# A Fourier mix in front of an MLP: the sum along the sequence of the third and fourth batch as a DFT of length six over the chunks

## The chip, the cores and the metric

The kernel runs on one core of one Trainium2 chip. The metric is the device time of one execution in microseconds. TensorE is called PE, VectorE DVE, ScalarE ACT, GpSimd POOL, and SyncE, which issues most transfers, SP.

## The reference

There are four batches. In each, a recurrent attention with decay (8 heads, 768 positions, 64 values a head) gives `x` of 768 x 512. Then comes a Fourier mix and an MLP:

```
X = np.fft.fft(x, axis=1)
X = np.fft.fft(X, axis=2)
u = x + np.real(X)
un = (u - mean(u)) / sqrt(var(u) + 1e-6)
out = u + relu(un @ w_ch1) @ w_ch2
```

The first transform runs along the 768 positions, the second along the 512 columns. The real part needs the cosine and the sine sums along the sequence, for frequencies 0 to 384; the others mirror them.

## The kernel before, in words

Position = 128 * chunk + row, with six chunks and the 128 rows on the partitions. `x16` holds x in f16, each chunk in two halves: columns 0 to 255 and columns 256 to 511 in reversed order, so that a column and its mirror stand at the same place.

**Attention of one batch** goes in steps over four pairs of heads. `cast_unit` (POOL), `t_unit` (transposes), `kv_unit` (products of keys and values, L683, and VectorE's running sums `s`, L693), `a_unit` (scores, PE L664; the mask is put on by VectorE, L667, giving `atm`, in three parts of two chunks) and `y_unit`: PE takes `s` (L714) and then `atm` (L718) into two PSUM banks, and ScalarE evicts them into `x16` (L726).

**The fold.** `fold_s` (L743) makes sums and differences of chunk c and chunk c + 3: `ab[:, parity, c, half, column]`. Even frequencies need the sums, odd ones the differences. It runs twice for a batch: on columns 0 to 129 of either half when the third pair of heads is done, on the rest after the fourth pair. `fold_d` (L770) folds the two halves into `eo` (sum for the cosine, difference for the sine), `fold_e` (L784, L786) folds once more into `ee`. What is left for each of the four column groups (`e` for cosine or sine, `cb`) is a sum over three chunks of 128 rows for each parity: `s1_unit` (L847) does it with three matmuls of 193 columns a parity, the tables `csp` and `ssp` on the moving side, into a PSUM bank of two blocks; ScalarE evicts the bank into `g`, putting even and odd frequencies in turn, and VectorE writes the mirror `gr` (L858). `g0_unit` (L874 to L900) makes the sum of column 0 by itself: two small VectorE operations, nine matmuls of 4 columns (L891), two small VectorE operations.

**The second transform and the norm.** `s2_unit` (L1009 to L1039) contracts `g` with tables along the columns for blocks `kb` of 128 frequencies, and `norm_unit` and `unT_unit` make the normalised, transposed input of the MLP.

**The MLP** is done in two halves `rt` of 384 positions: sixteen `h_unit` (four matmuls of 384 columns each, L1087, into one of three PSUM banks; the eviction with the Relu is on ScalarE, L1091, for the numbers in `ACT_ROWS`, else on VectorE, L1093), then three output blocks of sixteen matmuls (L1130), each evicted by VectorE (L1134) and sent out by SP.

**The order of the work.** The first batch up to its norm has an order written out by hand (`FIRST`). Behind that, `emit` merges streams of units: each stream has a start and an end on an axis on which batch b's MLP takes b to b + 1, its units are spread evenly between them, and all units are emitted by that place. The constants `DM1`, `TS1`, `DA1`, `LD1` give the starts and ends. While batch b's MLP runs, batch b + 1's attention, fold and first half of the mix run beside it. Each engine then takes its instructions strictly in the emitted order and waits for what each one needs.

Of the kernel before, what the change touches and what calls it, by code (L numbers as in the profile page):

```python
# [11 lines left out]
AF = mybir.ActivationFunctionType  # L12
# [7 lines left out]
P = 128  # L20
B, H, S, D = 4, 8, 768, 64
DM = 512
# [24 lines left out]
"""  # L47
ON_ACT = {'q': (0, 1, 0), 'kv': (1, 1, 1), 'g': (0, 1, 1), 'gr': (0, 0, 0)}
FB = 1
DM0, DM1 = (0.183, 0.205, 0.286, 0.408), (0.004, 0.137, 0.232, 0.341)  # L50
TS0 = (0.228, 0.358, 0.398, 0.465, 0.512, 0.573, 0.684, 0.694)
TS1 = (-0.040, -0.020, 0.048, 0.585)
DA0, DA1 = (0.043, 0.161, 0.176, 0.190, 0.284, 0.321), (0.063, 0.067, 0.063, 0.158, 0.168, 0.189)
LD0, LD1 = (0.223, 0.312), (-0.370, 0.140)
HT0 = (0.666, 0.693, 0.632, 0.590)
NPE = 2
KD = (2, 3)
NT = 0.6
ACT_ROWS = ((2, 5, 6, 7, 8, 9, 10, 14), (0, 3, 6, 7, 9, 10, 11, 12, 14, 15), (2, 4, 5, 6, 7, 8, 10, 11, 13, 14))


@with_exitstack
def kernel(
# [668 lines left out]
    def fold_s(b, lo, hi, s0, s1):  # L732
        def run():
            x = xts[b % 2]
            if b not in fd:
                fd[b] = dict(
                    ab=fp.tile([P, 2, 3, 2, XW], f16, tag="xab", name="xab"),
                    eo=fp.tile([P, 2, 2, 3, 256], f16, tag="eo", name="eo"),
                    g=gp.tile([P, 4, KN], f16, tag="g16", name="g16"),
                    gr=gp.tile([P, 4, 384], f16, tag="g16r", name="g16r"))  # L740
            ab = fd[b]["ab"]
            for a, op in ((0, ALU.add), (1, ALU.subtract)):
                nc.vector.tensor_tensor(out=ab[:, a, :, s0:s1, lo:hi],  # L743
                                        in0=x[:, 0:3, s0:s1, lo:hi],
                                        in1=x[:, 3:6, s0:s1, lo:hi], op=op)
        return run
# [18 lines left out]
    def fold_d(b, cb, es=(0, 1)):  # L765
# [7 lines left out]
                                        op=(ALU.add, ALU.subtract)[e])  # L773
        return run

    def fold_e(b, e):
        def run():
            eo = fd[b]["eo"]
            if e == 0:
                fd[b]["ee"] = fp.tile([P, 4, 2, 3, 128], f16, tag="xab", name="ee",  # L780
                                      padded_shape=[P, 4, 2, 3, 130])
            ee = fd[b]["ee"]
            lo, hi = eo[:, e, :, :, 0:128], eo[:, e, :, :, 254:126:-1]
            nc.vector.tensor_tensor(out=ee[:, 2 * e], in0=lo, in1=hi,  # L784
                                    op=ALU.add if e == 0 else ALU.subtract)
            nc.vector.tensor_tensor(out=ee[:, 2 * e + 1], in0=lo, in1=hi,  # L786
                                    op=ALU.subtract if e == 0 else ALU.add)
            if e == 0:
                nc.vector.tensor_copy(ee[:, 1, :, :, 127:128], eo[:, 0, :, :, 255:256])
        return run  # L790
# [49 lines left out]
    def s1_unit(b, e, cb):  # L840
        def run():
            eo, g, gr = fd[b]["eo"], fd[b]["g"], fd[b]["gr"]
            tab = csp if e == 0 else ssp
            ps = ps_g.tile([P, 2, NK], f32, tag="g", name="ps1", padded_shape=[P, 2, 256])
            for par in range(2):
                for sb in range(3):
                    nc.tensor.matmul(ps[:, par, :],  # L847
                                     fd[b]["ee"][:, 2 * e + cb, par, sb, :] if b >= FB else
                                     eo[:, e, par, sb, 128 * cb:128 * cb + 128],
                                     tab[:, par, sb, :], start=(sb == 0), stop=(sb == 2))  # L850
            gi = 2 * e + cb
            dst = g[:, gi].rearrange("p (i t) -> p t i", t=2)
            if e == 0 or ON_ACT["g"][min(b, 2)]:
                nc.scalar.copy(dst, ps)
            else:
                nc.vector.tensor_copy(dst, ps)
            if b:
                (nc.scalar.copy if ON_ACT["gr"][min(b, 2)] else nc.vector.tensor_copy)(  # L858
                    gr[:, gi], g[:, gi, 384:0:-1])
        return run  # L860
# [4 lines left out]
    def g0_unit(b, parts=(0, 1, 2)):  # L865
        def run():
            for part in parts:
                (g0_a, g0_b, g0_c)[part](b)
        return run
# [212 lines left out]
    def h_unit(b, rt, fb):  # L1082
        def run():
            unT = lb[b]["unT"]
            psh = ps_pm.tile([P, 384], f32, tag="pm", name="psh", padded_shape=[P, DM])
            for cb in range(4):
                nc.tensor.matmul(psh, w116[:, cb, fb * P:(fb + 1) * P],  # L1087
                                 unT[:, cb, rt * 384:(rt + 1) * 384],
                                 start=(cb == 0), stop=(cb == 3))
            if fb in ACT_ROWS[2 if (b, rt) == (B - 1, 0) else rt]:  # L1090
                nc.scalar.activation(ht16[:, fb, :], psh, AF.Relu, bias=0.0, scale=-1.0)  # L1091
            else:
                nc.vector.tensor_scalar(out=ht16[:, fb, :], in0=psh, scalar1=-1.0, scalar2=0.0,  # L1093
                                        op0=ALU.mult, op1=ALU.max)
        return run
# [61 lines left out]
    def attn_steps(b):  # L1157
        steps = []
        for step in range(6):
            un = []  # L1160
            if step < 4:
                un.append(held(cast_unit(b, step)))
            i = step - 1
            if 0 <= i < 4:
                un.append(kv_unit(b, i))
            i = step - 2
            if 0 <= i < 4:
                un.append(y_unit(b, i))
                if i == 2:
                    un += [fold_s(b, 0, 130, 0, 2), fold_d(b, 0)]  # L1170
                    if b < FB:
                        un += [g0_unit(b), s1_unit(b, 0, 0), s1_unit(b, 1, 0)]
            if step < 4:
                un.append(t_unit(b, step))
            i = step - 1
            if 0 <= i < 4:
                if b == 0:
                    un += [a0_unit(b, i, 0), a0_unit(b, i, 1)]
                else:
                    un += [a_unit(b, i, part) for part in range(3)]  # L1180
            if step == 5:
                un += [fold_s(b, 130, 258, 0, 2), fold_d(b, 1)]
                if b >= FB:
                    un += [g0_unit(b), fold_e(b, 0), fold_e(b, 1)]
            steps.append(un)
        return steps

# [88 lines left out]
    for b in range(B):  # L1276
        majors = []
        if b == 0:
            for kb in range(3):
                if kb:  # L1280
                    majors.append(unT_unit(0, kb))
                majors += [h0_unit(kb, g) for g in range(4)]
        else:
            majors += [h_unit(b, 0, fb) for fb in range(NFB)]
        majors.append(rstd_unit(b, 0))
        majors += [ch_unit(b, 0, rb3, part) for rb3 in range(3) for part in range(4)]
        majors += [h_unit(b, 1, fb) for fb in range(NFB)]
        majors.append(rstd_unit(b, 1))
        majors += [ch_unit(b, 1, rb3, part) for rb3 in range(3) for part in range(4)]
        streams.append((majors, b, b + 1.0))  # L1290
        streams += mix_units(b, [3, 4, 5], *(b + t for t in (DM0 if b == 0 else DM1)))
        if b + 1 < B:
            steps = attn_steps(b + 1)
            if b == 0:
                streams.append(([load_unit(1, i, 6) for i in range(4)], LD0[0], LD0[1]))
                streams.append(([qt_zeros], 0.1, 0.15))
                streams.append(([half_tables], HT0[0], HT0[1]))
                streams.append(([pad_unit], HT0[2], HT0[3]))
                ts = TS0
            else:  # L1300
                streams.append(([load_unit(b + 1, i) for i in range(4)], b + LD1[0], b + LD1[1]))
                n = [len(u) for u in steps[1:]]
                ts = list(TS1[:2]) + [TS1[2] + TS1[3] * sum(n[:j]) / sum(n) for j in range(6)]
            streams.append((steps[0], b + ts[0], b + ts[1]))
            streams += [(u, b + ts[j + 2], b + ts[j + 3]) for j, u in enumerate(steps[1:])]
            end = b + ts[-1]
            da = DA0 if b == 0 else DA1
            streams.append(([s1_unit(b + 1, e, cb) for cb in range(2) for e in range(2)
                             if cb or b + 1 >= FB], end + da[0], end + da[1]))
            streams += mix_units(b + 1, [0, 1, 2], *(end + t for t in da[2:]))  # L1310
# [31 lines left out]
```

## Time and profile before

| what | value |
|---|---|
| median of three runs | 242.17 us (241.97 to 242.35) |
| the profiled execution | 242.19 us |
| its span, first to last instruction | 240.2 us |
| PE busy | 228.5 us, 1999 matmuls |
| VectorE busy | 172.8 us |
| ScalarE busy | 120.8 us |
| granted TensorE clock, mean | 1.000 |

The profile has one row for each group of instructions, by line of the kernel before. The chain of waits is followed back from the last instruction: each piece has its start, its length and what ran. The timeline has start, length, engine, line and operation, and in brackets the idle time ahead and what ended it. Matmuls overlap, so that the mean of one is longer than the step from one to the next.

### The profile page before, as it was taken

To read this page: it belongs to the slowest core of one execution; us is meant where nothing else is said; L and a number is where in the kernel's file an instruction comes from. 1 tells how busy PE (TensorE), PEld (TensorE's weight loads), DVE (VectorE), ACT (ScalarE), POOL (GpSimd) and SP (SyncE) were. 2 spreads that over 40 slices of the span, in tenths; PEclk is the share of its full clock that TensorE was granted. 3 is DMA by queue.
4 is the path that set the end of the run, shared out by engine and by line. 5 is a ranking of instruction groups with operands and counts; after the bars stand their busy time and mean duration, and the time that the engine had idled before them with its cause. 6 is when DMAs were issued, how large, how long until landed. Compare 5 with 4: busy or idle time off the path is not lost.

```text
span 240.2 us, 5238 instructions
## 1 busy us (share of the span) xinstructions
PE 228.5 (95%) x1999; PEld 142.6 (59%) x1999; DVE 172.8 (72%) x419; ACT 120.8 (50%) x268; POOL 81.6 (34%) x148
## 2 busy tenths in 40 slices
PE   0888999999999999999999999999999999999994
PEld 0366779756774646665557446655675455446543
DVE  8789987968898789977995749977886557315121
ACT  5989759674865544941248406722366227203400
POOL 8377802675300097850001808930003224000000
PEclk9999999999999999999999999999999999999999
DMA  7999999999999399979999587675100331221012
GB/s 179 232 271 266 209 206 207 209 246 247 233 231 216 65 202 217 192 142 136 257 275 208 106 182 207 130 117 153 44 3 0 84 115 23 44 90 44 1 44 87
DMA packets 100808, 36.77 MB, mean 153 GB/s; under 512 B 91440, under 2 KB 97840, under 8 KB 100784
## 3 DMA queue, kind: packets, MB, share of 16 engines
q1 hardware_dynamic: 96560, 32.25, 63.7%
q0 software_dynamic: 4224, 4.19, 10.5%
q8 instruction: 15, 0.25, 0.4%
q14 instruction: 9, 0.07, 0.1%
HBM read 27.26 MB, written 6.29 MB: 140 GB/s over the span
## 4 chain that ended last, share of the span: by engine, by line
PE 83%; DVE 5%; SPq 5%; DMA 3%; POOL 2%; ACT 1%; issue 1%; ACTq 0%; POOLq 0%; DVEq 0%
PE psc L1130 34%; PE psh L1087 28%; SPq L216 5%; PE psh L1104 3%; PE wkA L664 3%; DMA q<-in_q_dram 3%; PE ps L847 3%; PE wkY L718 2%; PE pq L1009 2%; PE wkY L714 1%; PE wkK L683 1%; PE ps L827 1%; PE tq L620 1%; PE pst L1074 1%; DVE u L931 1%
## 5 line engine op out<-in xcount | busy, mean ns | idle before, releaser
L1130 PE MATMUL psc<-w,ht 128*128 128x512 f16 (+2 forms) x400 | 88.9, 370 | 0.0
L1087 PE MATMUL psh<-unT,w 128*128 128x384 f16 x448 | 81.6, 326 | 0.3 <-ACT ht L1091 0.3
L1130 PEld LDWEIGHTS <-ht 128*128 128x128 f16 x400 | 37.6, 98 | 36.8
L1087 PEld LDWEIGHTS <-w 128*128 128x128 f16 x448 | 42.1, 98 | 24.2 <-issue 0.8
L1091 ACT ACTIVATE ht<-psh 128x384 f16<-128x384 f32 x66 | 31.7, 490 | 41.2 <-PE psh L1087 40.3
L1037 POOL TENSOR_TENSOR u<-u,x 128x256 f32<-128x256 f32 x21 | 13.4, 636 | 107.1 <-DVE u L1016 95.0
L1134 DVE SCALAR_TENSOR_TENSOR ob<-psc,stats,u 128x512 f32<-128x512 f32 (+2 forms) x25 | 18.1, 724 | 29.0 <-PE psc L1130 28.9
L1093 DVE TENSOR_SCALAR ht<-psh 128x384 f16<-128x384 f32 x46 | 25.3, 549 | 8.9 <-PE psh L1087 8.5
L667 DVE TENSOR_TENSOR atm<-wkA,maskp 128x512 f16<-128x512 f32 x36 | 23.6, 681 | 1.5 <-PE wkA L664 1.5
L1051 ACT ACTIVATE un<-u,stats 128x512 f16<-128x512 f32 x21 | 14.8, 719 | 12.2 <-DVE stats L1050 8.2
L1049 DVE BATCH_NORM_STATS2 bst<-u 128x6 f32<-128x512 f32 x21 | 14.4, 687 | 4.9 <-POOL u L1039 4.7
L693 DVE SCALAR_TENSOR_TENSOR s<-s,gk,wkK 128x128 f16<-128x128 f16 x48 | 16.2, 337 | 2.4 <-ACT s L689 1.6
L726 ACT ACTIVATE x<-wkY,gexp 128x384 f16<-128x384 f32 x24 | 12.9, 581 | 9.0 <-PE wkY L718 8.9
L438 POOL TENSOR_SCALAR kd<-k,gexp 128x384 f16<-128x384 f32 x24 | 13.9, 589 | 3.4 <-DMA k<-in_k_dram 3.1
L1039 POOL TENSOR_TENSOR u<-u,x 128x256 f32<-128x256 f32 x21 | 13.3, 636 | 0.0
L664 PE MATMUL wkA<-qTz,kT 128*128 128x256 f16 x72 | 13.2, 272 | 0.1
L1011 ACT COPY qn<-pq 128x128 f32<-128x128 f32 x18 | 4.9, 274 | 13.7 <-PE pq L1009 13.6
L1104 PEld LDWEIGHTS <-w 128*128 128x128 f16 x192 | 11.0, 98 | 0.9 <-issue 0.5
L1104 PE MATMUL psh<-unT,w 128*128 128x128 f16 x192 | 11.4, 219 | 0.1
L1016 DVE SCALAR_TENSOR_TENSOR u<-pq,g,qn 128x256 f32<-128x256 f32 x18 | 8.5, 473 | 3.2 <-PE psh L1087 2.5
L443 POOL TENSOR_SCALAR v<-v 128x768 f16<-128x768 f32 x12 | 10.0, 834 | 1.5 <-DMA v<-in_v_dram 1.5
L664 PEld LDWEIGHTS <-kT 128*128 128x128 f16 x72 | 6.9, 98 | 5.6 <-issue 0.5
(175 smaller groups left out, 310.4 us busy)
## 6 DMA issues: line engine op xcount, KB each, us to landing
q<-in_q_dram SPq DMA_DIRECT2D x16, 384.0 KB, 6.0
k<-in_k_dram SPq DMA_DIRECT2D x16, 384.0 KB, 5.6
v<-in_v_dram SPq DMA_DIRECT2D x16, 384.0 KB, 6.2
out_dram<-ob SPq DMA_DIRECT2D x23, 256.0 KB, 2.4
w<-in_moe_w_ch_dram POOLq DMA_DIRECT2D x8, 512.0 KB, 10.7
unT<-un SPq DMA_TRANSPOSE x15, 2.4
out_dram<-ob SPq DMA_DIRECT2D x1, 192.0 KB, 1.9
kT<-kd SPq DMA_TRANSPOSE x10, 3.1
```

Source lines behind the costliest of these rows:

```text
L438: kc = nc.gpsimd.tensor_scalar(out=kd[:, :, h2, :], in0=k32[:, h2], scalar1=gkd[:, h0 + h2:h0 + h2 + 1], scalar2=1.0, op0=ALU.mult, op1=AL ...
L664: mm = nc.tensor.matmul(wk[:, c2], st["kT"][:, c, :], st["qT"][:, :, c, :], start=True, stop=True)
L667: nc.vector.tensor_tensor(out=st["atm"][:, 2 * part:2 * part + 2], in0=wk, in1=maskp[:, PAIR_ORDER[i]].unsqueeze(1).to_broadcast([P, 2, 2, ...
L693: nc.vector.scalar_tensor_tensor(out=s16[:, c], in0=s16[:, c - 1], scalar=gk2[:, hp:hp + 1], in1=wk[:, c - c0], op0=ALU.mult, op1=ALU.add)
L1049: nc.vector.bn_stats(bst, u[:, kb, :])
L1051: nc.scalar.activation(un, u[:, kb, :], AF.Identity, bias=stats[:, kb, 0:1], scale=-1.0)
L1087: nc.tensor.matmul(psh, w116[:, cb, fb * P:(fb + 1) * P], unT[:, cb, rt * 384:(rt + 1) * 384], start=(cb == 0), stop=(cb == 3))
L1091: nc.scalar.activation(ht16[:, fb, :], psh, AF.Relu, bias=0.0, scale=-1.0)
L1093: nc.vector.tensor_scalar(out=ht16[:, fb, :], in0=psh, scalar1=-1.0, scalar2=0.0, op0=ALU.mult, op1=ALU.max)
L1104: mm = nc.tensor.matmul(psh[:, f], w116[:, cb, fb * P:(fb + 1) * P], unT[:, cb, kb * P:(kb + 1) * P], start=(cb == 0), stop=(cb == 3))
L1130: nc.tensor.matmul(psc[:, c0:c1], ht16[:, fb, rb3 * P:(rb3 + 1) * P], w216[:, fb, c0:c1], start=(fb == 0), stop=(fb == NFB - 1))
L1134: nc.vector.scalar_tensor_tensor(out=ob[:, c0:c1], in0=psc[:, c0:c1], scalar=lb[b]["st"][:, rb, 3:4], in1=lb[b]["u"][:, rb, c0:c1], op0=AL ...
```

## The change

For the third and fourth batch (`b >= SIX`, SIX = 2) the sum over the three folded chunks is taken apart once more. A frequency is k = 6 j + r. `fold_six` makes, from the three chunks a0, a1, a2 of `ab`, for each parity: a1 + a2, a1 - a2, twice a0 minus or plus one of these, and a0 plus or minus the same. It runs on one half of the columns at a time, between `fold_s` and `fold_d`, with six VectorE operations (two sums of 512 elements, two scalar-tensor operations and two sums of 256) and one ScalarE copy of 256. `fold_d` then waits for that copy.

After it, the frequencies with r = 0 (even) or 3 (odd) need only the first of the three chunks, 65 or 64 of them, and the other two residues of a parity, 2 x 64 together, need the second and the third. So `s1_unit` still has six matmuls for each column group, but of 65, 128, 128 and 64, 128, 128 columns instead of six of 193. They write straight to the place of the frequency in the bank, which is every sixth float for one residue and two of each six for a pair. Eviction and mirror read 385 dense floats. The tables for the second and third chunk are made by `six_table`, sixteen ScalarE operations behind the second batch's first half of the MLP, in place of the two chunks of `csp` and `ssp` that are no longer read. `g0_unit` of these batches is split: its first part stands ahead of `fold_six`, which overwrites `ab`.

Along with it several places on the axis are changed, and `ACT_ROWS`: in the first half of the MLP eleven evictions on ScalarE instead of eight, in the second nine instead of ten, in the last batch's first half eight instead of ten.

In the emitted order PE then has 16 matmuls L1130 instead of 12 between the third pair's L718 and the fourth pair's first scores, and 42 L1087 instead of 36 between the fourth pair's last L718 and the first sequence sum. On VectorE, an output eviction (L1134) stands behind the first L743 where it stood ahead of it, then the six of `fold_six`, the first third of `atm`, L770, the second third, an output eviction, the last third.

```
-DM0, DM1 = (0.183, 0.205, 0.286, 0.408), (0.004, 0.137, 0.232, 0.341)
+DM0, DM1 = (0.183, 0.205, 0.286, 0.408), (-0.008, 0.133, 0.238, 0.436)
-TS1 = (-0.040, -0.020, 0.048, 0.585)
+TS1 = (-0.033, 0.032, 0.052, 0.580)
-DA0, DA1 = (0.043, 0.161, 0.176, 0.190, 0.284, 0.321), (0.063, 0.067, 0.063, 0.158, 0.168, 0.189)
+DA0, DA1 = (0.043, 0.161, 0.176, 0.190, 0.284, 0.321), (0.024, 0.070, 0.093, 0.201, 0.202, 0.232)
-ACT_ROWS = ((2, 5, 6, 7, 8, 9, 10, 14), (0, 3, 6, 7, 9, 10, 11, 12, 14, 15), (2, 4, 5, 6, 7, 8, 10, 11, 13, 14))
+ACT_ROWS = ((0, 1, 2, 5, 6, 7, 8, 9, 10, 13, 14), (0, 3, 6, 7, 9, 10, 11, 12, 15), (3, 4, 5, 7, 8, 10, 11, 13))
...
+    def six_of(par):
+        return [t[:, par, 1:3].rearrange("p c k -> p (c k)") for t in (csp, ssp)]
+
+    def six_table(e, par):
...
+                with tc.issue_after(lb[SIX - 1]["relu"].ins):
+                    nc.scalar.activation(out, in_, AF.Copy, bias=0.0, scale=m)
...
+    def fold_six(b, half):
+        def run():
+            ab, eo = fd[b]["ab"], fd[b]["eo"]
+            c0 = 2 + 128 * half
+            a = [ab[:, :, c, :, c0:c0 + 128] for c in range(3)]
+            t = ab[:, :, 0, :, 2:130] if half else eo[:, 0, :, 0:2, 128:256]
+            nc.vector.tensor_tensor(out=t, in0=a[1], in1=a[2], op=ALU.add)
+            nc.vector.tensor_tensor(out=a[2], in0=a[1], in1=a[2], op=ALU.subtract)
+            for par, z, op, inv in ((0, t, ALU.subtract, ALU.add),
+                                    (1, a[2], ALU.add, ALU.subtract)):
+                (nc.gpsimd if SIXP else nc.vector).scalar_tensor_tensor(
+                    out=a[1][:, par], in0=a[0][:, par], scalar=2.0,
+                                               in1=z[:, par], op0=ALU.mult, op1=op)
+                nc.vector.tensor_tensor(out=a[0][:, par], in0=a[0][:, par], in1=z[:, par], op=inv)
+            nc.scalar.copy(a[2][:, 1], t[:, 1])
...
     def s1_unit(b, e, cb):
...
+            if b >= SIX:
+                ps = ps_g.tile([P, KN - 1], f32, tag="g", name="ps1", padded_shape=[P, DM])
+                by6 = ps[:, 0:384].rearrange("p (j r) -> p j r", r=6)
+                for par in range(2):
+                    z, to = fd[b]["ee"][:, 2 * e + cb, par], six_of(par)[e]
+                    two = by6[:, :, 1:6:4] if par else by6[:, :, 2:5:2]
+                    for sb, (o, out) in enumerate(((0, by6[:, :, 3] if par else ps[:, 0:385:6]),
+                                                   (65, two), (193, two))):
+                        w = 128 if sb else 65 - par
+                        nc.tensor.matmul(out, z[:, sb, :], to[:, o:o + w],
+                                         start=par == sb == 0, stop=par == 1 and sb == 2,
+                                         skip_group_check=True)
...
             if step == 5:
-                un += [fold_s(b, 130, 258, 0, 2), fold_d(b, 1)]
+                un.append(fold_s(b, 130, 258, 0, 2))
+                if b >= SIX:
+                    un += [g0_unit(b, (0,)), fold_six(b, 1)]
+                un.append(fold_d(b, 1))
                 if b >= FB:
-                    un += [g0_unit(b), fold_e(b, 0), fold_e(b, 1)]
+                    un += [g0_unit(b, (1, 2) if b >= SIX else (0, 1, 2)), fold_e(b, 0),
+                           fold_e(b, 1)]
```

More of the change, by code (lines that the diff above doesn't have):

```diff
@@ L56 @@
 NPE = 2
+SIX = 2
+SIXP = 0
+ST0 = (1.30, 1.5)
 KD = (2, 3)
 NT = 0.6
-ACT_ROWS = ((2, 5, 6, 7, 8, 9, 10, 14), (0, 3, 6, 7, 9, 10, 11, 12, 14, 15), (2, 4, 5, 6, 7, 8, 10, 11, 13, 14))
+ACT_ROWS = ((0, 1, 2, 5, 6, 7, 8, 9, 10, 13, 14), (0, 3, 6, 7, 9, 10, 11, 12, 15), (3, 4, 5, 7, 8, 10, 11, 13))
 @with_exitstack
@@ L774, in fold_d, with run @@
         return run
+    def six_of(par):
+        return [t[:, par, 1:3].rearrange("p c k -> p (c k)") for t in (csp, ssp)]
+    def six_table(e, par):
+        def run():
+            same, other = (csp, ssp) if e == 0 else (ssp, csp)
+            sg = (-1.0 if e == 0 else 1.0) * math.sqrt(0.75)
+            to = six_of(par)[e]
+            src, alt = (t[:, par, 0, 0:192].rearrange("p (j r) -> p r j", r=3)
+                        for t in (same, other))
+            r0, r1 = ((1, 2), (0, 2))[par]
+            pairs = [to[:, o:o + 128].rearrange("p (j r) -> p r j", r=2) for o in (65, 193)]
+            one = same[:, 0, 0, 0:193:3] if par == 0 else src[:, 1]
+            for out, in_, m in ((to[:, 0:65 - par], one, 1.0),
+                                (pairs[0], src[:, r0:r1 + 1:r1 - r0], 0.5),
+                                (pairs[1][:, 0], alt[:, r0], sg),
+                                (pairs[1][:, 1], alt[:, r1], -sg)):
+                if SIX > 1:
+                    with tc.issue_after(lb[SIX - 1]["relu"].ins):
+                        nc.scalar.activation(out, in_, AF.Copy, bias=0.0, scale=m)
+                else:
+                    nc.gpsimd.tensor_scalar(out=out, in0=in_, scalar1=m, scalar2=1.0,
+                                            op0=ALU.mult, op1=ALU.mult)
+        return run
+    def fold_six(b, half):
+        def run():
+            ab, eo = fd[b]["ab"], fd[b]["eo"]
[11 more added lines that the diff above has]
+            nc.scalar.copy(a[2][:, 1], t[:, 1])
+        return run
     def fold_e(b, e):
@@ L843, in run @@
             tab = csp if e == 0 else ssp
+            if b >= SIX:
[10 more added lines that the diff above has]
+                                         skip_group_check=True)
+                gi = 2 * e + cb
+                (nc.scalar.copy if e == 0 or ON_ACT["g"][min(b, 2)] else nc.vector.tensor_copy)(
+                    g[:, gi, 0:KN - 1], ps)
+                (nc.scalar.copy if ON_ACT["gr"][min(b, 2)] else nc.vector.tensor_copy)(
+                    gr[:, gi], g[:, gi, 384:0:-1])
+                return
             ps = ps_g.tile([P, 2, NK], f32, tag="g", name="ps1", padded_shape=[P, 2, 256])
@@ L1090, in run @@
             if fb in ACT_ROWS[2 if (b, rt) == (B - 1, 0) else rt]:
-                nc.scalar.activation(ht16[:, fb, :], psh, AF.Relu, bias=0.0, scale=-1.0)
+                relu = nc.scalar.activation(ht16[:, fb, :], psh, AF.Relu, bias=0.0, scale=-1.0)
+                if rt == 0:
+                    lb[b]["relu"] = relu
             else:
@@ L1169, in attn_steps @@
                 if i == 2:
-                    un += [fold_s(b, 0, 130, 0, 2), fold_d(b, 0)]
+                    un += [fold_s(b, 0, 130, 0, 2)]
+                    if b >= SIX:
+                        un.append(fold_six(b, 0))
+                    un.append(fold_d(b, 0))
                     if b < FB:
@@ L1181, in attn_steps @@
             if step == 5:
-                un += [fold_s(b, 130, 258, 0, 2), fold_d(b, 1)]
+                un.append(fold_s(b, 130, 258, 0, 2))
+                if b >= SIX:
+                    un += [g0_unit(b, (0,)), fold_six(b, 1)]
+                un.append(fold_d(b, 1))
                 if b >= FB:
-                    un += [g0_unit(b), fold_e(b, 0), fold_e(b, 1)]
+                    un += [g0_unit(b, (1, 2) if b >= SIX else (0, 1, 2)), fold_e(b, 0),
+                           fold_e(b, 1)]
             steps.append(un)
@@ L1298 @@
                 streams.append(([pad_unit], HT0[2], HT0[3]))
+                streams.append(([six_table(e, par) for e in range(2) for par in range(2)], *ST0))
                 ts = TS0
```

## The prediction

> **What bounds the kernel now.** I read the page first, then who waits for whom on PE, the busy time by stretch, the chain of waits and the VectorE timeline around the fold of the third batch.
>
> ```profile
> span 240.2 us, 5238 instructions
> PE 228.5 (95%) x1999; PEld 142.6 (59%) x1999; DVE 172.8 (72%) x419; ACT 120.8 (50%) x268; POOL 81.6 (34%) x148
> ```
> ```profile
> PE psh L1087 <- ACT ht L1091: 0.3, 1, 0.3
> ```
> ```profile
> PE ps L891 <- DVE xg L882: 0.2, 1, 0.2
> ```
> ```profile
> 113.00:120.00 7.00, 6.94 (x77) 4.14 (x74) 6.58 (x13) 1.69 (x4) 0.00 (x0) 1.00 1.06 229
> ```
> PE is busy for 95% of the span, and behind the first batch its list of waits holds only the two short ones shown. So from then on the time is the sum of the PE instructions, in their fixed order: a nanosecond less on PE is a nanosecond less, and a PE wait is paid in full. The last row is the stretch in which the third batch is folded for the first time: PE 6.94 of 7.00 us, VectorE 6.58 of 7.00 (third figure), clock 1.00. Two engines are full at once there.
>
> The chain through that stretch, and VectorE in the same one:
>
> ```profile
> 113.01 0.29 PE wkY L714 x10
> 113.31 0.35 PE wkY L718 x12
> 113.66 2.59 PE psc L1130 x12
> 116.25 0.06 issue
> 116.31 0.38 PE wkA L664 x2
> 116.69 0.86 PE psc L1130 x4
> 117.55 0.22 PE wkA L664 x2
> 117.77 0.65 PE psh L1087 x4
> 118.42 0.22 PE wkA L664 x2
> 118.64 0.65 PE psh L1087 x4
> 119.29 0.29 PE wkY L714 x10
> 119.58 0.42 PE wkY L718 x12
> 120.00 4.48 PE psh L1087 x27
> 124.47 0.22 PE ps L891 x9
> 124.70 1.49 PE psh L1087 x9
> 126.18 2.05 PE ps L847 x24
> ```
> ```profile
> 114.60 1.04 DVE L743 TENSOR_TENSOR xab<-x 128x780 f16<-128x780 f16 x2 [0.16 <-ACT x L726]
> 115.68 1.03 DVE L770 TENSOR_TENSOR eo<-xab 128x768 f16<-128x768 f16 x2
> 116.73 0.69 DVE L667 TENSOR_TENSOR atm<-wkA,maskp 128x512 f16<-128x512 f32 x1
> 117.59 0.75 DVE L1134 SCALAR_TENSOR_TENSOR ob<-psc,stats,u 128x512 f32<-128x512 f32 x1 [0.17 <-PE psc L1130]
> 118.26 1.28 DVE L667 TENSOR_TENSOR atm<-wkA,maskp 128x512 f16<-128x512 f32 x2
> ```
> ```profile
> 124.17 0.56 DVE L784 TENSOR_TENSOR ee<-eo 128x768 f16<-128x768 f16 x1
> ```
> What to see: the wkY L718 at 119.58 read the three masked scores (atm, L667), and VectorE ends the third at 118.26 + 1.28 = 119.54. That is 0.04 us before they are wanted; their x12 take 0.42, not the 0.35 of 113.31. The fourth batch has the same order:
>
> ```profile
> 169.99 1.28 DVE L667 TENSOR_TENSOR atm<-wkA,maskp 128x512 f16<-128x512 f32 x2
> ```
> ```profile
> 171.31 0.42 PE wkY L718 x12
> ```
> There the third ends at 171.27, and the wkY L718 stand at 171.31. VectorE is just in time in both batches.
>
> **The change, part by part.**
>
> *The sequence sums (L847).* 24 matmuls of 193 columns in each batch, 2.05 us, become 24 of 65, 128, 128, 64, 128, 128 columns, four times: 8 short, 16 of 128. The count and the weight loads stay; 4632 columns become 2564. New is that each writes columns that lie 2 to 6 floats apart in PSUM. Prices:
>
> ```profile
> L714 PE MATMUL wkY<-s,qTz x120: 189/193/193, 59.3 to 171.1; 128*128 128x64 f16 x120
> ```
> ```profile
> L683 PE MATMUL wkK<-v,kd x60: 217/219/219, 54.0 to 163.9; 128*128 128x128 f16 x60
> ```
> ```profile
> L550 PE MATMUL wkK<-v,kd x40: 216/247/348, 12.0 to 25.2; 128*64 128x64 f16 x40
> ```
> ```profile
> 25.01 0.40 PE wkK L550 x10
> ```
> ```profile
> 111.87 0.28 PE wkK L683 x5
> ```
> Dense columns: 64 cost 0.29/10 = 0.029 us (L714 at 113.01), 128 cost 0.28/5 = 0.056. Then a batch needs 8 x 0.029 + 16 x 0.056 = 1.13 us, 0.92 less than now. The only matmuls here that spread their columns are L550 (every fifth float). With 64 columns they last 247 ns in the median, not the 193 of 64 dense columns, and more than the 219 of 128. They differ in one more way (weights of 64 columns, two side by side), so this row doesn't settle it. By the chain five such pairs take 0.40, 0.08 each. I take two columns' time for each spread column: 64 cost what 128 dense do (0.056), 128 what 256 do (0.22/2 = 0.11, the wkA at 117.55): 8 x 0.056 + 16 x 0.11 = 2.21, **0.16 more** than now. The ends are 0.92 less, and 8 x 0.08 + 16 x 0.16 = 3.20, 1.15 more. I take the middle since it is nearest to the one row that has the spread.
>
> The Trainium skill, page "SBUF — State Buffer", section "Door 1: The DMA port swizzle", speaks against this part: PSUM has lines of 8 bytes, two fp32 values, and any access that isn't contiguous slows matmuls significantly. By that rule the 0.92 would be lost, and the sum would be the one with 0.16; L550 agrees in direction.
>
> *fold_six on VectorE.* Six operations for each half: two sums of 512 elements, two scalar-tensor ones of 256, two sums of 256, and a copy on ScalarE. No row has these sizes in f16; the nearest:
>
> ```profile
> L770 DVE TENSOR_TENSOR eo<-xab 128x768 f16<-128x768 f16 x12 | 6.1, 552 | 0.1
> ```
> ```profile
> L760 DVE TENSOR_TENSOR xab<-x 128x384 f16<-128x384 f16 x6 | 1.9, 357 | 0.3 <-ACT x L596 0.2
> ```
> ```profile
> L693 DVE SCALAR_TENSOR_TENSOR s<-s,gk,wkK 128x128 f16<-128x128 f16 x48 | 16.2, 337 | 2.4 <-ACT s L689 1.6
> ```
> ```profile
> L1019 DVE SCALAR_TENSOR_TENSOR u<-pq,g,qn 128x256 f32<-128x256 f32 x18 | 8.5, 473 | 0.0
> ```
> A straight line through 357 and 552 ns gives 422 for 512 and 292 for 256 elements; for the scalar-tensor one I take 400, between 337 and 473. Sum 2 x (422 + 400 + 292) = 2.23 us. Two unconnected operations overlap by 0.08 (two of 0.56 take 1.04 at 114.60); a dependent one starts some 0.04 after the end (115.64 to 115.68). Most of the six depend on the one before. I take **2.1 us** for a half; the ends are 1.5 (all overlapped, the scalar-tensor ones as quick as sums) and 2.6 (473, none overlapped).
>
> *First half: what waits.* In the changed order VectorE does, behind L743: an output sum (L1134, it stood ahead before), fold_six, the first atm, L770, the second atm, an output sum, the third atm. L770 also waits for ScalarE's copy; that lies under the first atm (0.64), ScalarE being idle there, and if it didn't, the two atm and the output sum behind L770 would be late by as much. From 114.60: L743 to 115.68, L1134 0.67 (117.59 to 118.26), fold_six 2.1, atm 0.64, L770 1.05, atm 0.64, L1134 0.67, atm 0.68: 122.1. PE has more between, too: 16 psc for 12 (+0.86), 4 psc for 4 psh (+0.21), less the 0.22 that the first wkA and the issue lost (0.06 + 0.38 - 0.22). So wkY L718 are due at 119.58 + 0.85 = 120.43, and those of the last third four matmuls later, 120.55. They come at 122.1: PE stands **1.55 us**, in each of the two batches (0.95 to 2.05 with fold_six at its ends).
>
> *Second half.* Now the ee operations open the sequence sums: the first ended at 124.17 + 0.56 = 124.73, for sums that PE started at 126.18. After the change VectorE has fold_six (2.1), one more eviction L1093 (0.47, next to next) and the gm operation (0.1) ahead: 127.40. PE has 42 psh for 36, 6 x 1.49/9 = 1.0 more: due at 127.18. Late by 0.22, with the signal **0.25** (0 to 0.75). If the sums were quick, the second group would wait again, 0.2.
>
> *The rest.* The sixteen small table writes stand on ScalarE behind the second batch's evictions of its first half, in three parts of five, four and seven, with a cast of s (L689) and the x evictions between. At the cast's own 0.27 they take 4.3 us.
>
> ```profile
> 112.12 0.27 ACT L689 CAST s<-wkK 128x128 f16<-128x128 f32 x1 [4.30 <-issue]
> ```
> ScalarE stood idle for 4.30 us just ahead of this cast, and the four copies of fold_six fall where it is busy 1.69 of 7 us (the row of 113:120): cost nothing. Without that cover the cast, and the sums of s that VectorE makes of it, would come late by what stands ahead of it, 5 x 0.27 = 1.4. The evictions of h that change engines cancel (six leave VectorE, six come). The nine L891 of the second batch stand two psc later, so their 0.15 of the wait of 0.2 goes; VectorE's fold is what is late next, by one eviction, still in time. Where SP's queue changes places (transposes of un and k, an output against a load of v), each still stands a whole step ahead of its use; no PE wait names a DMA there, and I count 0. The ScalarE wait of 0.3 in the last batch I leave in.
>
> *Sum.* Each batch 1.55 + 0.25 + 0.16 = 1.96; twice 3.92, less 0.15: +3.77. The profiled execution took 242.19 us (its span 240.2 and 2.0 around it), the median of the runs is 242.17. Forecast **246.0**.
>
> **The rivals.**
>
> *Spread columns at full rate, VectorE late all the same.* For it: L550 differs in its weights too. Each batch 1.55 + 0.25 + 0.2 - 0.92 = 1.08; 242.19 + 2.16 - 0.15 = 244.2.
>
> *Faster: VectorE is in time and the columns are full rate.* For it: PE, which is the bound, has 45% fewer columns in this step. Against it: the stretch 113:120 had 0.4 us of VectorE left, and 2.8 us come in against 0.85 on PE. It would be 242.19 - 1.84 - 0.15 = 240.2. It decides at fold_six = 1.5 us: there the first wait of 0.95 just eats the 0.92.
>
> *The change doesn't do what it says on PE, and nothing waits*: spread columns at half rate, 2 x 0.16 - 0.15, 242.4. That needs VectorE to be free, and only costs.
>
> *Spread columns as dear as the pairs of L550*: 2 x (1.55 + 0.25 + 1.15) - 0.15, 247.9.
>
> **How the numbers follow.** Forecast 0.45, late with full rate 0.28, dear columns 0.08, faster 0.10, no gain and no wait 0.05, others 0.04. The forecast with fold_six at its ends goes from 244.3 to 248.0, the full-rate case from 242.1 to 246.2. The range 243.0 to 248.2 holds the forecast and the dear columns whole and some four fifths of the full-rate case. A measurement of this kernel can tell about 0.2% (0.5 us) from no change. Faster gets 0.10 and a little of the full-rate case; same the 242.4 and its like, 0.06; slower 0.83.
>
> **What would show it.** PE's waits would name DVE atm (L667) ahead of wkY L718, 1.5 us, twice, and DVE ee ahead of the new sums. Those sums would last some 219 and 272 ns (half rate) or 193 and 219 (full). VectorE's total would rise from 172.8 by four times 2.2 to some 181.7. The forecast is wrong if fold_six takes under 1.5 us, or the third atm comes ahead of its wkY.

## The result, and the profile after

The changed kernel takes 245.95 us (median of 5 runs, 245.84 to 246.02) against 241.97 for the kernel before it on the same chip: a ratio of 1.0161, 95% interval 1.0146 to 1.0176. It is slower by 4.0 us; the forecast was 246.0. The total fits. The terms do not all fit, and that is the subject of what follows.

The page of the changed kernel (profiled execution 246.02 us):

```profile
span 244.0 us, 5281 instructions
PE 229.9 (94%) x1999; PEld 142.6 (58%) x1999; DVE 179.5 (74%) x443; ACT 124.8 (51%) x288; POOL 81.7 (33%) x148
```
The span grew by 3.8 us, PE's busy time by 1.4. The rest is time in which PE stood. Who let it stand, from PE's list of waits (total, times, longest); behind the first batch these two are the only ones of 0.2 or more, and before the change neither was there:

```profile
PE psh L1150 <- DMA unT<-un: 1.3, 1, 1.3
PE wkA L667 <- DMA qTz<-q16z: 0.9, 1, 0.9
```
Line numbers are now those of the changed kernel, except in rows of before. psh and psc are the MLP's two products, wkA the scores, wkY the attention's sums; qTz, kT and unT are the transposed q, k and input of the MLP. Both waits are for transposing DMAs, to which the prediction gave 0. Their places on PE's timeline (start, duration, count):

```profile
105.24 1.89 PE L1195 MATMUL psc<-w,ht 128*128 128x512 f16 x8
107.99 0.38 PE L667 MATMUL wkA<-qTz,kT 128*128 128x256 f16 x2 [0.86 <-DMA qTz<-q16z]
...
140.83 3.40 PE L1195 MATMUL psc<-w,ht 128*128 128x512 f16 x15
145.49 1.47 PE L1150 MATMUL psh<-unT,w 128*128 128x384 f16 x8 [1.26 <-DMA unT<-un]
```
Matmuls overlap in these rows: a wkA lasts 272 ns, and two of them take 0.22 in the chain. So the gaps are measured by the rate of the stream (0.86 for four psc, 0.216 each): the first eight were over at 105.24 + 1.73 = 106.97, and PE lost 1.02; the fifteen at 140.83 + 3.23 = 144.06, and PE lost 1.43. Together 2.45 us.

SP's queue shows where these transfers stand. Beside the second batch's MLP (before, then after) and beside the third's (after):

```profile
102.89 1.51 SPq L609 DMA_TRANSPOSE qTz<-q16z  x1
104.50 2.81 SPq L1070 DMA_TRANSPOSE unT<-un  x2
```
```profile
99.48 2.63 SPq L1133 DMA_TRANSPOSE unT<-un  x2
102.21 1.23 SPq L614 DMA_TRANSPOSE kT<-kd  x1
103.53 1.46 SPq L612 DMA_TRANSPOSE qTz<-q16z  x1
...
140.50 0.53 SPq L1203 DMA_DIRECT2D out_dram<-ob  x1
141.13 1.47 SPq L612 DMA_TRANSPOSE qTz<-q16z  x1
142.69 1.56 SPq L1133 DMA_TRANSPOSE unT<-un  x1
```
In the kernel before, two unT follow this qTz; in the changed one two stand ahead of kT and qTz, which is issued 0.64 later. PE also wants it earlier: the same wkA stood at 108.63 before (chain) and is due at 106.97 after, 1.66 earlier.

```profile
108.63 0.22 PE wkA L664 x2
```
The chain after gives the landing of the two late ones:

```profile
103.53 4.32 DMA qTz<-q16z
...
142.69 2.76 DMA unT<-un
```
From issue to landing 4.3 and 2.8 us. From its issue to the time at which PE was due qTz had 106.97 - 103.53 = 3.44 us, and unT 144.06 - 142.69 = 1.37: standing "a whole step ahead of its use" wasn't early enough.

The late unT has two parts. Its input `un` comes from ScalarE:

```profile
139.77 0.72 ACT L1114 ACTIVATE un<-u,stats 128x512 f16<-128x512 f32 x1 [1.05 <-POOL q16z L438]
```
It is ready at 140.49, where the last `un` of this batch was ready at 138.05 before (136.72 + 1.33). Then an output and a qTz stand ahead on SP until 142.69. To land in time it had to be issued by 144.06 - 2.76 = 141.30. No run changed one of the two alone, so their shares stay open.

The stretch that the prediction worked out, the first and second half of the third batch's fold, on PE:

```profile
119.79 0.57 PE L721 MATMUL wkY<-v,atm 128*128 128x64 f16 x8
120.19 0.98 PE L1150 MATMUL psh<-unT,w 128*128 128x384 f16 x5
121.26 0.29 PE L721 MATMUL wkY<-v,atm 128*128 128x64 f16 x4
121.39 3.25 PE L1150 MATMUL psh<-unT,w 128*128 128x384 f16 x19
124.72 0.38 PE L954 MATMUL ps<-xg,csn 128*128 128x4 f16 x9
```
Eight wkY take 0.23 at full rate and took 0.40 to the next start: 0.17 lost, going by the times to the second atm, which ends at 119.95 (119.27 + 0.68). Five psh at 0.163 end at 121.00; the last four wkY start at 121.26: 0.26 lost. Nineteen psh end at 124.48; g0's matmuls start at 124.72: 0.24 lost. The fourth batch has the same rows (last four wkY at 175.37, g0 at 178.83) with the same gaps. VectorE beside it:

```profile
115.75 0.41 DVE L810 TENSOR_TENSOR eo<-xab 128x512 f16<-128x512 f16 x1
...
117.73 0.68 DVE L670 TENSOR_TENSOR atm<-wkA,maskp 128x512 f16<-128x512 f32 x1
...
120.53 0.68 DVE L670 TENSOR_TENSOR atm<-wkA,maskp 128x512 f16<-128x512 f32 x1
```
fold_six stands between the first two rows, 117.73 - 115.75 = 1.98 us, and the third atm ends at 121.21, 0.05 ahead of the wkY at 121.26: there VectorE is what ended PE's wait. And the sums, by the chain, and one matmul of them (mean ns is the last figure before the idle time):

```profile
128.86 0.55 PE ps L898 x6
...
129.90 1.65 PE ps L898 x18
```
```profile
L898 PE MATMUL ps<-csp,ee 128*128 128x128 f16 x8 | 1.4, 307 | 0.0
L898 PE MATMUL ps<-csp,ee 128*128 128x64 f16 x2 | 0.5, 261 | 0.0
```
2.20 us for the 24, where the 24 wider ones took 2.05.

So the account: transfers 2.45, second and third atm 2 x 0.43, g0 2 x 0.24, sums 2 x 0.15, together 4.1; less 0.3, since the ScalarE wait of the last batch, which the forecast had left in, is gone from the list. That is 3.8, the growth of the span. Smaller gaps elsewhere are not in it; by the same measure they come to about 1 us in either trace (after, 0.28 each in front of a psh at 102.67 and of a wkY at 155.69; before, 0.22 in front of the wkA at 116.31), and nearly balance.

### The profile page after: what moved, and what is told of

The parts are those of the page before. It is cut to its first block, busy times and chain, and to the rows that moved or that the text cites. A ratio compares the mean times of both kernels' runs of the same rounds, so it can differ in the third digit from the quotient of the medians.

```text
span 244.0 us, 5281 instructions
## 1 busy us (share of the span) xinstructions
PE 229.9 (94%) x1999; PEld 142.6 (58%) x1999; DVE 179.5 (74%) x443; ACT 124.8 (51%) x288; POOL 81.7 (33%) x148
## 4 chain that ended last, share of the span: by engine, by line
PE 64%; DVE 15%; POOL 7%; DMA 6%; issue 3%; ACT 2%; SPq 1%; POOLq 0%; DVEq 0%
PE psc L1195 25%; PE psh L1150 20%; PE psh L1169 3%; DMA v<-in_v_dram 3%; DVE atm L670 2%; PE wkA L667 2%; PE ps L898 2%; DMA qTz<-q16z 2%; POOL u L1102 2%; PE ps L872 1%; PE wkY L721 1%; DVE xab L746 1%; DVE ob L1199 1%; DVE ht L1158 1%; PE pq L1072 1%
```

## The experiments

The change is two things in one diff: another computation, and four lists of places (DM1, TS1, DA1, ACT_ROWS). Theory **V**: VectorE's fold_six is late for PE, as the prediction had it, and costs nearly all of the time. Theory **S**: the new places, by way of SP's queue, cost what the late transfers show, and the computation only its sums and small waits. All are timed in 3 rounds beside the kernel before. The first four ran on a chip where that took 242.40 us in the median (241.87 to 243.7), the others where it took 242.1; to compare across, the ratios are used.

**The places without the computation.** Before's fold, with the changed kernel's places:

```
-SIX = 2
+SIX = 4
...
-                streams.append(([six_table(e, par) for e in range(2) for par in range(2)], *ST0))
```


> The kernel before with only the new places on the axis and the new division of evictions; no six-length fold. Theory V (VectorE: fold_six is what costs, as predicted): 241.8 us, the kernel before less the 0.15 of its one short wait. Theory S (the new places issue the transposes late, as the two waits for transfers of 1.3 and 0.9 us in the trace of the changed kernel suggest): those waits are there without fold_six too, 243.0 to 244.4 us.

Measured: 244.57 us, ratio 1.0088 (1.0057 to 1.0118). The places alone cost 2.1 us, where V had none. PE's list (of the slowest of the five executions, 245.48) has the late unT of the third batch again, and qTz with 0.3:

```profile
PE psh L1150 <- DMA unT<-un: 1.3, 1, 1.3
```

**The computation with before's places.** The changed kernel with DM1, TS1, DA1 and ACT_ROWS put back.

> The changed kernel with the places and the division of evictions of the kernel before. Theory V: VectorE is as late as now or later, 245.5 us or more. Theory S: the two waits for transfers (1.02 and 1.43 us between matmuls) go, the 0.66 a batch behind VectorE and the 0.15 a batch of the sequence sums stay: 243.5 us.

Measured: 243.75 us, ratio 1.0059 (1.0042 to 1.0077); no transfer is left in PE's list. Here qTz is issued 2.5 us earlier than in the changed kernel:

```profile
100.99 2.23 SPq L612 DMA_TRANSPOSE qTz<-q16z  x1
```
Computation alone 0.59%, places alone 0.88%, both 1.61%: some 1.4, 2.1 and 3.9 us of 242.1. S holds, and the two nearly add up.

**VectorE's share.** The changed kernel without the body of fold_six (six VectorE operations and a ScalarE copy):

```
     def fold_six(b, half):
...
-            nc.vector.tensor_tensor(out=t, in0=a[1], in1=a[2], op=ALU.add)
-            nc.vector.tensor_tensor(out=a[2], in0=a[1], in1=a[2], op=ALU.subtract)
...
-            nc.scalar.copy(a[2][:, 1], t[:, 1])
```


> The changed kernel with the six VectorE operations and the ScalarE copy of fold_six left out (the sums are then made of unfolded chunks); all else stands. Theory V: both waits behind VectorE go, 2 x 1.8, 242.3 us. Theory S: only 2 x 0.66 go, 244.6 us, and the waits for transfers stay.

Measured: 246.05 us, ratio 1.015 (1.0115 to 1.0184). Leaving out four times 2 us of VectorE work brings nothing that this measurement can tell from the 1.0161 of the changed kernel, and both theories missed: S had given it the small waits. The waits for transfers stay at 1.3 and 0.9, and a wait for the third atm stays too:

```profile
118.97 0.75 DVE ob L1190
119.72 0.61 DVE atm L670
```
The chain shows the place: an output sum stands ahead of that atm on VectorE, and itself waited for PE's psc. Without fold_six another operation is late there. But PE's order is another too: the twelve wkY stand together, where the changed kernel has five psh in front of the last four.

```profile
119.93 0.77 PE L721 MATMUL wkY<-v,atm 128*128 128x64 f16 x12
```
So this run doesn't take fold_six away alone, and it leaves open how much of the small waits is fold_six's. V, by which fold_six costs nearly all of the time, falls already by the two runs before.

**The columns.** The changed kernel with each matmul of the sums writing adjacent PSUM columns (the order of the frequencies is then another):

```
-                    for sb, (o, out) in enumerate(((0, by6[:, :, 3] if par else ps[:, 0:385:6]),
-                                                   (65, two), (193, two))):
+                    d0 = 193 * par
+                    one, two = ps[:, d0:d0 + 65 - par], ps[:, d0 + 65 - par:d0 + 193 - par]
+                    for sb, (o, out) in enumerate(((0, one), (65, two), (193, two))):
```


> The changed kernel with each sequence sum written to dense columns of its bank, so that the frequencies stand in another order; counts, weights and widths stay. If the spread columns halve the rate: the block of 24 goes from 2.20 to about 1.13 us, of which 0.2 a batch may come back as a wait for the ee operations: 243.8 to 244.3 us. If the widths or weights set the 2.20: no change, 245.9 us.

Measured: 244.54 us, ratio 1.0089 (1.0055 to 1.0123). Same widths, same weights, same count:

```profile
L899 PE MATMUL ps<-csp,ee 128*128 128x128 f16 x8 | 0.9, 221 | 0.0
```
```profile
129.14 0.30 PE ps L899 x6
```
221 ns for 307, and 0.30 us for 0.55: nothing but the spread of the columns differs in these six. By the ratio the time is 244.1 of the 241.97 of the first comparison, within the forecast; the quicker sums run into the late ee again, 0.16 a batch. That is the measurement which the row of L550 in the prediction couldn't give. The rule of the Trainium skill weighed there (page "SBUF — State Buffer", section "Door 1: The DMA port swizzle") agrees, and these rows put a number to it.

**Dense columns, and the order put right in the eviction.** Before's places, a block of 65 columns for each residue of the frequency, tables laid to match; ScalarE's eviction reads in order and writes every sixth f16:

```
-                    two = by6[:, :, 1:6:4] if par else by6[:, :, 2:5:2]
+                    two = ps[:, 1:6:4] if par else ps[:, 2:5:2]
...
-                    g[:, gi, 0:KN - 1], ps)
+                    g[:, gi].rearrange("p (j r) -> p r j", r=6), ps)
```


> The DFT of length six with the places that before gave its units (DM1, TS1, DA1, ACT_ROWS of before), and the sums written to dense PSUM columns: each residue of the frequency has a block of 65 columns, the tables of the pairs are laid residue by residue, and the ACT eviction puts 390 columns back into order. Stated for a chip on which before takes 242.4. If spread columns are what the fold costs beside its places, the run with before's places (243.75) loses 8 blocks at about 0.55 against 0.30, that is 2.0, and gets back the wait for ee of about 0.16 a batch that the slow blocks had covered: 242.0 (241.6 to 242.4), blocks of about 0.30 and 128-column matmuls near 221 ns. If it is VectorE's later work that decides, the faster sums only run into the late ee: 243.4 or more, with a wait for ee in front of the sums of 0.5 or more a batch.

Measured: 253.99 us, ratio 1.0482 (1.0445 to 1.0518): 12 us from the forecast, and neither theory had the reason. It is the eviction, for which PE now waits:

```profile
L902 ACT CAST g<-ps 128x390 f16<-128x390 f32 x4 | 5.6, 1589 | 0.3 <-PE ps L898 0.3
```
```profile
PE pq L1072 <- ACT g L902: 6.0, 4, 2.4
```
The second loss is in the clock. In the stretches below PE's busy time comes first, PEclk stands third from the end:

```profile
130.00:132.00 2.00, 0.00 (x0) 0.00 (x0) 0.26 (x1) 2.00 (x3) 0.00 (x0) 0.90 1.35 221
132.00:138.00 6.00, 5.05 (x22) 2.68 (x23) 3.73 (x9) 3.79 (x10) 2.46 (x4) 0.50 0.35 77
138.00:140.00 2.00, 2.00 (x9) 0.84 (x8) 1.72 (x5) 0.72 (x1) 1.83 (x4) 0.89 0.00 0
```
In a wait of 2.4 us PE fell to half the clock, for some 6.8 us (0.4 at the end of the first row, 6, and 0.4 of the third); four psh there take 1.28 us in the chain, not 0.65.

**The same, written in order.** One statement differs: the eviction reads PSUM at a stride of 65 columns and writes adjacent f16.

```
-                    g[:, gi].rearrange("p (j r) -> p r j", r=6), ps)
+                    g[:, gi].rearrange("p (j r) -> p j r", r=6),
+                    ps.rearrange("p r j -> p j r"))
```


> As the dense sums with before's places, but the ACT eviction walks in the order of the output: it reads PSUM at a stride of 65 columns and writes adjacent f16, where the other read PSUM in order and wrote every sixth f16 (1589 ns where 385 spread columns took 483). If the scattered write is what cost, the eviction takes about 490 ns, the waits of 2.4 and 0.6 a batch in front of the mix go, and the time is 242.0 (241.6 to 242.6) where before is 242.1. If any permutation costs it (the strided read as well), the eviction stays at 1.4 or more and the time at 253 to 254.

Measured: 242.46 us (242.14 to 242.67, 10 runs), ratio 1.0011 (1.0002 to 1.0021), as the first case of the forecast had it.

```profile
L902 ACT CAST g<-ps 128x390 f16<-128x390 f32 x4 | 1.7, 490 | 0.4 <-PE ps L898 0.3
```
```profile
127.36 0.30 PE ps L898 x6
127.67 0.49 PE psh L1151 x3
128.15 1.06 PE ps L898 x18
```
The same permutation costs nothing on the reading side: 490 ns, where the 385 spread columns took 483 in the changed kernel. The sums take 1.36 us, 0.69 less than the kernel before, 1.4 in two batches. That this isn't a gain is due to waits of PE. PE stands for VectorE 0.14 to 0.26 each time, 1.3 in the two batches: at the second and last third of the wkY, at g0, and now in front of the second group of sums (three psh from 127.50 are over at 127.99, the sums start at 128.14). It also stands 0.25 a batch in front of the second transform, where it needs ScalarE's evictions of g, and 0.29 in front of the wkA of pair 3. So here VectorE's work does cost: with places and columns out of the way, its waits are nearly as long as what PE saves. This is read from the trace; no run took these waits out of this version.

**Moving VectorE's steps.** Two attempts to remove these waits. On the version with the scattered eviction, fold_six and fold_d of the first half behind the masks of pair 3, and g0's matmuls behind fold_e:

```
                     un += [a_unit(b, i, part) for part in range(3)]
+                    if i == 3 and b >= SIX:
+                        un += [fold_six(b, 0), fold_d(b, 0)]
```


> As the run with before's places and dense columns, and two steps moved behind others on VectorE: fold_six and fold_d of the first half stand behind the three masks of pair 3, and g0's matmuls behind the folds fold_e. If the waits of PE left in this stretch (0.14 and 0.26 at the last wkY, 0.24 at g0, a batch) come from VectorE's order, they go: about 0.6 a batch, some 1 us off the run beside it, 241.0 (240.6 to 241.6). If they only move on (ee later, a transfer wanted earlier because PE's order changes with it), no change against the run beside it within 0.4, with the same length of gaps at other lines.

Measured: 255.47 us, ratio 1.0533 (1.0486 to 1.058). The late eviction is all there is to see in it, so it doesn't bear on the question, save that qTz was late by 1.0 in front of wkA. Then on the fold with before's places and spread columns, only fold_d moved, and g0 likewise:

> The length-six fold with before's places (243.75 in its run), and two steps moved on VectorE: fold_d of the first half behind the three masks of pair 3, g0's matmuls behind fold_e. If PE's small waits there (0.14 and 0.26 at the last wkY, 0.24 at g0, a batch) come from VectorE's order, they go: 242.6 (242.2 to 243.2). If the planner's other order brings wkA of pair 3 forward by four psc matmuls and qTz is then late, the gap there grows from 0.14 to 0.5 or more, and the time is 243.5 to 244.0.

Measured: 243.54 us, ratio 1.0057 (1.0037 to 1.0077), not to be told from the run without the move (1.0059); the span is 241.5 us, there 241.9. The small waits at the last wkY and at g0 went, and the one in front of wkA of pair 3 grew, as the second case had it: PE takes it earlier, and qTz is not there.

```profile
PE wkA L667 <- DMA qTz<-q16z: 0.6, 1, 0.6
```

**Which of the places.** The changed kernel with some of before's lists. First DM1 and DA1, then TS1:

> After with DM1 and DA1 of before alone (TS1 and ACT_ROWS stay new). If the late unT of the third batch (PE's gap of 1.43 in after) comes from the new places of the attention steps in DA1 and of the mix in DM1, the wait for unT goes and the one for qTz (1.02) stays: 244.6 (244.2 to 245.2) where after is 246.0. If the late transfers come from TS1, or from SP's queue as the two tables of transfers make it together, the wait for unT stays at 1.3 in PE's list and the time at 246.0.

Measured: 245.93 us, ratio 1.0158 (1.0119 to 1.0198). The wait for unT fell, the time didn't: the ScalarE wait of the last batch (0.3) is back, and the one for qTz stays.

```profile
PE wkA L667 <- DMA qTz<-q16z: 0.7, 1, 0.7
PE psh L1150 <- DMA unT<-un: 0.5, 1, 0.5
```


> After with TS1 of before alone (DM1, DA1 and ACT_ROWS stay new): kT and qTz are issued at before's places, ahead of the two unT. If the late qTz (PE's gap of 1.02 in after) comes from TS1, its wait goes and the one for unT (1.43) stays: 245.0 (244.6 to 245.4). If it comes from the earlier place that PE's order gives wkA of pair 2 (DA1), the wait stays at 0.9 and the time at 246.0.

Measured: 246.2 us, ratio 1.0158 (1.0116 to 1.02); both waits as in the changed kernel, 1.3 and 1.0. TS1 isn't it. Then all three, with only ACT_ROWS new:

> After with DM1, DA1 and TS1 of before (ACT_ROWS stays new). Neither table alone moved the qTz; with all four constants of before the wait was gone. If the two tables work only together (the mix's transposes and the attention's pass through one queue), both waits for transfers are gone: 243.9 (243.5 to 244.4) with SP's order unT, qTz, kT, unT, unT. If it is ACT_ROWS, through the engine that makes ht and what is queued behind it, the waits of 0.9 for qTz and some 0.5 for unT stay and the time is 245.9.

Measured: 245.8 us, ratio 1.0147 (1.0132 to 1.0163). Against my guess, the list that says which engine evicts h decides, with the other three at before's: between this run and the one at 1.0059 only ACT_ROWS differs. qTz is still behind the second unT, and late:

```profile
PE wkA L667 <- DMA qTz<-q16z: 1.2, 1, 1.2
```
Last, ACT_ROWS of before alone:

> After with ACT_ROWS of before alone (DM1, DA1 and TS1 stay new). Built so, SP's queue of the second batch has qTz and kT ahead of the two last unT again, and nothing else in that queue changes; the third batch's unT still stands behind an output and a qTz. If the place in SP's queue is what made qTz late, PE's gap of 1.02 in front of wkA goes, the one of 1.43 in front of psh stays, and the time is 245.0 (244.6 to 245.4). If ACT_ROWS costs by itself what the step from the run with three old tables to the one with four gained (2.0), whatever the queue, it is 244.0 and the gap for unT is gone as well. If it only acts together with the tables, it is 246.0.

Measured: 246.08 us, ratio 1.0161 (1.014 to 1.0182). qTz is issued ahead of the last two unT again, 2.8 us earlier than in the changed kernel, and its wait is gone from the list, as forecast. The time isn't lower:

```profile
100.71 1.80 SPq L612 DMA_TRANSPOSE qTz<-q16z  x1
```
```profile
106.66 0.22 PE wkA L667 x2
```
```profile
PE psh L1150 <- DMA unT<-un: 1.5, 1, 1.5
PE psh L1150 <- ACT ht L1154: 1.1, 2, 0.9
```
PE takes the wkA at 106.66 (chain), as early as the changed kernel wanted it, without a wait. What was saved there went to a longer wait for unT and, in the last batch, to ScalarE's evictions of h, two waits of 1.1 together. So, with PE at the wkA as early as that, the place in SP's queue is shown as the cause of the late qTz; the 2.5 us of the places is no sum of parts. Only with all four lists put back do the waits go together. Other than the part on the kernel before says, then, the places on the axis alone don't fix the order of the queue; by what rule it follows from ACT_ROWS is open. So is whether the dense version with its last waits removed would pass the kernel before: no run tried that.

## Why the prediction was right, and where it was not

*PE is the bound, and its waits are paid in full*: right. The 3.8 us of the span are found on PE, with the smaller gaps left aside.

*The sums, +0.16 a batch*: right, 2.20 for 2.21. The single durations named as a mark, 272 and 219 ns, were not: 307 and 261. The block's length goes by the rate, two columns' time for each spread column, and the run with adjacent columns shows it.

*fold_six, 2.1 us*: 1.98; the straight line gave 422 and 292 for sums that took 421 and 282, and the scalar-tensor ones took 416 to 424 for 400. VectorE's total went to 179.5, not 181.7; a rise of 6.7 is less than four times 1.98, and what else became shorter wasn't followed up.

*First half, 1.55 a batch*: mis-sized, 0.43. The step that failed is the time at which the last third of the wkY is due, 120.55, right behind the other eight. PE takes five psh in between (0.81), and it was due at 121.00. Also the third atm came at 121.21, not 122.1: fold_s (L746) ended 0.47 earlier than its like before, the output sum behind it overlapped it by 0.08 where the sum put it behind its end, and from there to the end of the third atm VectorE took 6.12 us, not 6.45. The mechanism, VectorE late for the wkY, is there, at a quarter of the size.

*Second half, 0.25*: 0.24, but in another place. The sums did not wait for ee. g0's matmuls waited for the second xg operation, which has fold_six's first operation ahead of it:

```profile
124.19 0.34 DVE xab L810
124.53 0.15 DVE xg L945
```
This gap had been sized at nothing, the other at 0.25; that they agree is chance.

*SP's queue, 0*: wrong, 2.45. "Each still stands a whole step ahead of its use" looked at the order and not at the times: PE at the wkA 1.66 earlier, the last `un` 2.4 later, and 4.3 and 2.8 us to landing. It is the largest single term of the result, and the prediction had none for it.

*Less 0.15 for g0 of the second batch, ScalarE's 0.3 left in*: of small weight. The first went down by 0.18 by the rate of the stream (0.32 to 0.14); the latter went.

So the forecast of 246.0 came from 3.1 us of late masks, of which 0.9 exist, and from none of the 2.45 of late transfers. The two errors nearly cancel: that the total fits so closely is luck. The sign was safe in either account, since each term was a loss. Of the rivals, full-rate columns are excluded by the 307 ns, dear columns by the 2.20.

## What to carry to other kernels

When a diff moves steps as well as changes them, run each half by itself: here the fold cost 1.4 us, the places 2.1, and neither could be read from the total. For a transfer whose place in its queue changes, or whose use moves forward, take the time of use less the time from issue to landing, by the longest landing in the trace, not the order of the queue. When a result has to be permuted, let the eviction read at a stride and write in order; here matmuls that wrote spread columns paid nearly double, and an eviction that wrote scattered f16 three times.

## What the runs showed of the hardware that was not expected

- A spread PSUM column costs a matmul two columns' time: 24 matmuls of 64 to 128 columns 2.20 us, against 0.30 for six adjacent ones where six spread took 0.55.
- A ScalarE eviction of 390 columns takes 490 ns when it reads PSUM at a stride of 65 floats and writes adjacent f16, and 1589 ns when it reads in order and writes every sixth f16; the one that writes every second (386 columns, L917) takes 600. The Trainium skill, page "SBUF — State Buffer", section "Door 1: The DMA port swizzle", gives SBUF lines of 16 bytes and a penalty for each access that goes to a new one; by that figure a step of 12 bytes does so at most accesses, and these rows agree in direction.
- PE's clock fell to 0.50 in a wait of 2.4 us, 0.4 ahead of 132 and so some 1.7 us after the last matmul (129.95), and stayed there for some 6.8; over a gap of 1.43 us it stayed at 1.00 in the changed kernel:

```profile
145.00:150.00 5.00, 4.51 (x37) 3.02 (x38) 1.93 (x6) 2.52 (x8) 1.57 (x3) 1.00 0.82 225
```
The Trainium skill, page "TensorE: Matmul & The Clock Gate", section "Why this matters for your kernels", advises against gaps above some 3 us; here a shorter one was enough, and the measurement decides.
